# A pair's value product in three pieces among the scores, and fixed first-key tiles

## Chip, core and metric

The kernel runs on one core of a Trainium2 chip. The metric is device time in microseconds (us); lower is better. The engines of a core are TensorE (PE, matrix products; its weight loads are listed apart as PEld), VectorE (DVE), ScalarE (ACT), GpSimd (POOL) and SyncE (SP, which issues the DMAs here). Each engine works through its own list of instructions strictly in order and waits on semaphores for the others.

## What is computed

Three stages, all in float32; the attention stage is the one that the change touches.

```python
def _attn_ref(q, k, v, s):                 # q, k, v: (4, 8, 576, 64); s: (4, 8, 576)
    B, H, S, D = q.shape
    scores = q @ k.transpose(0, 1, 3, 2) / np.sqrt(D)
    causal = np.triu(np.ones((S, S), dtype=bool), k=1)
    cum = np.cumsum(np.maximum(s, 0.0), axis=-1)
    bias = -(cum[:, :, :, None] - cum[:, :, None, :])
    scores = np.where(causal, -1e9, scores + np.minimum(bias, 0.0))
    attn = softmax(scores)                 # max taken off, exp, divided by the row sum
    return attn @ v
# x = attn_out as (4, 576, 512)
# x = x + (u * (w_sg @ layernorm(v) + b_sg)) @ w_out, with (u, v) = gelu(x @ w_in)     (576, 1024)
# theta = x @ w_theta;  y = w_tok_r @ (x cos theta) + w_tok_i @ (x sin theta)
# out = (x + y) + relu((x + y) @ w_ch)
```

## The kernel before

**Stages.** The 32 heads (4 batches of 8) are worked through one after another by `attention`. After the eighth head of a batch, the first part of the feed-forward network of that batch (`ffn`) becomes the filler: `pace` emits pieces of it between the units of the next batch's heads, in proportion to their estimated cost in ns. So the first eight heads run without a filler (except loads of its weights), heads 8 to 31 with one. After head 31 come the rest of the network, the products with w_out, theta and the token mixing.

**One head.** A head has 576 queries in five tiles (0 to 4; tile 0 has 64 of its own) and the keys that each may see. `split_head` scales q and splits q and k into a rounded part and a remainder (tiles qA, kA, qB, kB; POOL, ACT and DVE share this work, and DMAs put the remainder and two rows of the running sum `cum` into qB and kB). `score_units` makes the scores of query tiles 0 to 3 in PSUM tiles of one bank (tag sc, four buffers) and those of tile 4 in a PSUM tile of two banks (sc2, one buffer, 288 columns used in each bank); then DVE takes the negated row maximum and ACT the exponential into E, with the row sums. `transpose_units` transposes E on PE (fifteen 128-column transposes in four PSUM tiles T, tag sc) and copies it out: the keys 0 to 63 to E0, the others to Ef. The product with the first key tile runs over 68 rows, of which rows 64 to 67 of E0 are zero; POOL sets them (L317) for every head, in a tile taken from a rotation of four.

**A pair.** Two heads share a tile of v. `pv_units` of an odd head makes the product of the pair: `R` and `R0` are the reciprocal row sums `Rb`, spread over the partitions by five transposes (ACT copies them to xT); `Y` (one bank) collects five key tiles for the queries 64 to 575, `Z` (64 columns) the one key tile of the first 64 queries. `pair` issues each product twice, once per head, the first head to the PSUM partitions 0 to 63 and the second to 64 to 127: the two are halves of the array that belong together. The five products of Y have 512, 512, 384, 128 and 256 columns. R0 and Z lie in spare columns of the last T. DVE multiplies Y and Z into xT (L376, L375), and `finish_pair` stores it and splits it for the network.

**What sets the order.** `ORDER` gives the units of one head in the order in which they are written: s a unit of scores of head g, t a unit of transposes of head g-1, p the split of head g+2 and the loads of head g+4; after them, in an even head, comes the whole `pv_units` of the pair before. When the kernel is built, a scheduler then puts each engine's instructions into a fixed order by their priority (the place in the program) and its own idea of when inputs and buffers are there. What runs is that order. The profile cuts buffer numbers and some endings from names: `sc` stands for sc and sc2, `E` for E and E0, `Q` and `K` for the loaded heads, and R0 and Z appear as T.

```python
    ORDER = "ssstsstspttt"
```

## Time and profile before

| | before |
|---|---|
| median of 3 runs | 723.15 us (719.99 to 725.91) |
| the profiled execution | 726.0 us |
| its span, first to last instruction | 723.9 us |
| PE, DVE, ACT, POOL busy in the span | 94%, 67%, 52%, 35% |
| mean granted TensorE clock | 0.983 of full speed |

The profile is of one execution, 0.4% above the median. A share of busy time is an average over stages: in the first 110 us there is no filler, from there to some 377 us attention and the network run together, then comes the change-over to the later stages.

### The profile page before, as it was taken

How to read it: one execution, taken by the hardware profiler on the slowest of the kernel's cores; microseconds unless marked ns; L12 is line 12 of the kernel's file. 1: busy time of each engine (PE TensorE's matmuls, PEld its weight loads, DVE VectorE, ACT ScalarE, POOL GpSimd, SP SyncE). 2: the span in 40 equal slices, each digit the busy share in tenths (PEclk: the TensorE clock that was granted, in tenths of full speed). 3: DMA queues.
4: the chain of work that ended last, by engine and by line, in shares of the span. 5: the costliest groups of instructions: out<-in, count | busy, mean ns of one | idle time of the engine just before them, and what ended most of it. 6: DMA issues, size and time to landing. Idle time of an engine off the chain costs nothing.

```text
span 723.9 us, 12514 instructions
## 1 busy us (share of the span) xinstructions
PE 678.8 (94%) x4496; PEld 593.8 (82%) x4496; DVE 486.4 (67%) x914; ACT 379.9 (52%) x888; POOL 254.0 (35%) x289
## 2 busy tenths in 40 slices
PE   6898978999999999999999687898999999999998
PEld 4676656888779878887788687887999989999997
DVE  5577979655659466675558899799876378457522
ACT  3567667764567734677436534566654056147100
POOL 6356544645326444454436654335000010010000
PEclk9999989999999999999999989999999999999999
DMA  5656763424332244321123578983100300300101
GB/s 143 192 158 186 202 174 91 114 73 141 108 99 78 77 122 144 110 69 42 42 93 119 176 240 260 326 290 124 66 1 1 132 1 1 126 6 1 66 1 65
DMA packets 50093, 80.76 MB, mean 112 GB/s; under 512 B 7248, under 2 KB 18768, under 8 KB 50032
## 3 DMA queue, kind: packets, MB, share of 16 engines
q1 hardware_dynamic: 50032, 79.97, 35.7%
q8 instruction: 35, 0.57, 0.3%
q14 instruction: 26, 0.21, 0.1%
HBM read 56.19 MB, written 19.02 MB: 104 GB/s over the span
## 4 chain that ended last, share of the span: by engine, by line
PE 60%; DVE 10%; DMA 4%; POOL 2%; issue 2%; ACT 2%; SPq 0%; DVEq 0%; POOLq 0%; ACTq 0%
PE yo L90 16%; PE fo L90 13%; PE co L90 7%; PE Y L90 6%; PE th L90 5%; PE sc L90 5%; PE T L329 4%; PE wo L90 2%; DVE wta L449 1%; DVE wta L451 1%; DMA x2d<-xr 1%; DMA x2T<-x2d 1%; DVE wta L448 1%; POOL vT L549 1%; DVE qA L245 1%
## 5 line engine op out<-in xcount | busy, mean ns | idle before, releaser
L282 ACT ACTIVATE E<-sc,negm 128x448 f32<-128x448 f32 (+4 forms) x160 | 84.2, 528 | 52.0 <-DVE negm L281 51.2
L281 DVE TENSOR_REDUCE negm<-sc 128x1 f32<-128x448 f32 (+4 forms) x160 | 74.2, 481 | 40.2 <-PE sc L90 39.0
L90 PE MATMUL yo<-wkh,zh 128*128 128x288 f32 x288 | 85.2, 296 | 0.1
L90 PE MATMUL yo<-wkl,zh 128*128 128x288 f32 x288 | 84.9, 296 | 0.0
L90 PE MATMUL yo<-wkh,zl 128*128 128x288 f32 x288 | 84.8, 296 | 0.0
L329 PE MATMUL T<-ident,E 128*128 128x128 f32 (+1 forms) x480 | 68.9, 277 | 3.3 <-ACT E L282 2.1
L90 PE MATMUL sc<-kA,qA 128*128 128x320 f32 (+3 forms) x192 | 63.0, 342 | 7.0 <-DVE Ef L335 3.2
L90 PE MATMUL sc<-kB,qB 68*128 68x320 f32 (+2 forms) x192 | 61.1, 328 | 6.6 <-DMA qB<-cd 3.1
L83 POOL TENSOR_SCALAR xt<-x2s 128x128 fp32r<-128x128 f32 x16 | 11.4, 725 | 136.7 <-PE tp L702 73.6
L90 PE MATMUL fo<-x,wih 128*128 128x288 f32 x256 | 58.4, 308 | 0.0
L329 PEld LDWEIGHTS T<-ident,E 128*128 128x128 f32 (+1 forms) x480 | 52.9, 133 | 6.4 <-ACT E L282 2.6
L245 DVE SCALAR_TENSOR_TENSOR qA<-Q,qA 64x576 fp32r<-64x576 f32 x32 | 48.5, 1516 | 10.5 <-POOL qA L243 9.8
L90 PEld LDWEIGHTS yo<-wkh,zh 128*128 128x128 f32 x288 | 54.1, 188 | 0.7 <-DVE x2T L775 0.4
L90 PEld LDWEIGHTS yo<-wkl,zh 128*128 128x128 f32 x288 | 53.9, 188 | 0.3
L90 PEld LDWEIGHTS yo<-wkh,zl 128*128 128x128 f32 x288 | 53.9, 188 | 0.1
L87 POOL TENSOR_TENSOR kB<-K,kA 64x576 fp32r<-64x576 f32 x32 | 49.9, 1559 | 8.9 <-ACT kA L79 7.2
L90 PE MATMUL co<-u,wch 128*128 128x288 f32 x256 | 52.9, 295 | 0.0
L90 PEld LDWEIGHTS sc<-kA,qA 128*128 128x128 f32 x192 | 37.1, 199 | 18.3 <-issue 5.6
L90 PE MATMUL wo<-gh,woh 128*128 128x288 f32 x128 | 39.8, 314 | 12.9 <-DVE xr L679 8.4
L90 PE MATMUL Y<-Ef,vr 128*64 128x128 f32 (+3 forms) x256 | 50.9, 439 | 0.0
L90 PEld LDWEIGHTS sc<-kB,qB 68*128 68x128 f32 x192 | 38.7, 202 | 9.2 <-issue 4.3
L317 POOL MEMSET E<- 4x576 f32 x32 | 17.4, 575 | 79.8 <-PE T L90 79.8
(172 smaller groups left out, 1938.4 us busy)
## 6 DMA issues: line engine op xcount, KB each, us to landing
Q<-in_q SPq DMA_DIRECT2D x64, 144.0 KB
K<-in_k SPq DMA_DIRECT2D x64, 144.0 KB
qB<-qA SPq DMA_DIRECT2D x32, 144.0 KB
xd<-xT SPq DMA_DIRECT2D x16, 288.0 KB
gd<-uT SPq DMA_DIRECT2D x16, 288.0 KB
gr<-gd SPq DMA_DIRECT2D x16, 288.0 KB
xr<-xd SPq DMA_DIRECT2D x16, 288.0 KB
x2d<-xr SPq DMA_DIRECT2D x16, 288.0 KB
```

What stands on the lines that cost most here:

```text
L83: nc.gpsimd.tensor_scalar(out, src, 1.0, 1.0, op0=ALU.mult, op1=ALU.mult)
L87: e.tensor_tensor(out, a, f32(hi), op=ALU.subtract)
L90: self.nc.tensor.matmul(out, lhsT, rhs, start=start, stop=stop)
L245: nc.vector.scalar_tensor_tensor(qA[64:128, :], Q2[64:128, :], 0.125, f32(qA[64:128, :]), op0=ALU.mult, op1=ALU.subtract)
L281: nc.vector.tensor_reduce(negm[0:rows, col:col + 1], o, axis=ax, op=ALU.max, negate=True)
L282: nc.scalar.activation(out, o, AF.Exp, bias=negm[0:rows, col:col + 1], accum_out=sm[0:rows, j, col:col + 1])
L317: nc.gpsimd.memset(E0[64:68], 0.0)
L329: nc.tensor.transpose(T[0:n, col:col + P], E[:, c:c + n], self.ident)
L448: nc.vector.tensor_scalar(ta.bitcast(U32), ta.bitcast(U32), 3, None, op0=ALU.logical_shift_left)
L449: nc.vector.scalar_tensor_tensor(ta.bitcast(U32), Hi, 0x80000000, ta.bitcast(U32), op0=ALU.bitwise_and, op1=ALU.bitwise_or)
L451: nc.vector.scalar_tensor_tensor(ta.bitcast(U32), L, 29, ta.bitcast(U32), op0=ALU.logical_shift_right, op1=ALU.bitwise_or)
L549: nc.gpsimd.tensor_scalar(vT[0:r, t], vT[0:r, t], rs[0:r, t:t + 1], nm[0:r, t:t + 1], op0=ALU.mult, op1=ALU.add)
```

## The change

The product of a pair moves from behind the even head that follows the pair to within the odd head after that, and is cut in three pieces, which `ORDER_V` places as v: R with its copy; the first two key tiles of Y; and R0, Z and the other three key tiles. The last pair of each batch stays where it was, in one go. R0 and Z now lie in spare columns (from 320) of the two banks of the head's own sc2 tile instead of in T. E0 is four fixed tiles; their rows 64 to 67 are set to zero once, by DVE, at the start, and the POOL instructions for it go.

```diff
+    ORDER_V = "sssvtsvstspvttt"
...
+        self.E0 = [self.a1.tile([P, S], F32, name=f"E0{i}") for i in range(4)]
...
+        for e in self.E0:
+            nc.vector.memset(e[64:68, :], 0.0)
...
-        o = self.psS.tile([P, 2, 512], F32, name="sc2", tag="sc2", bufs=1)
+        o = self.wide = self.psS.tile([P, 2, 512], F32, name="sc2", tag="sc2", bufs=1)
...
-        E0 = self.a2.tile([P, S], F32, name="E0", tag="E0", bufs=4)
+        E0 = self.E0[g % 4]
...
-        nc.gpsimd.memset(E0[64:68], 0.0)
...
     def pv_units(self, g):
...
-        R, R0 = self.psS.tile([P, 512], F32, name="R", tag="sc"), T[:, 384:512]
-        for t in range(5):
-            col = (t - 1) % 5
-            o = R0 if t == 0 else R[:, QS[t] - 64:QS[t] + 64]
-            nc.tensor.transpose(o, Rb[:, col].rearrange("p j d -> p (j d)"), self.ident)
-        nc.scalar.copy(xT[:, 512:576], R0[:, 0:64])
+        R = self.psS.tile([P, 512], F32, name="R", tag="sc")
+
+        def spread(o, t):
+            nc.tensor.transpose(o, Rb[:, (t - 1) % 5].rearrange("p j d -> p (j d)"), self.ident)
+
+        for t in range(1, 5):
+            spread(R[:, QS[t] - 64:QS[t] + 64], t)
         nc.scalar.copy(xT[:, 0:512], R)
-        yield 400.0
-
-        Y, Z = self.psS.tile([P, 512], F32, name="Y", tag="sc"), T[:, 320:384]
+        yield 300.0
+        Y = self.psS.tile([P, 512], F32, name="Y", tag="sc")
...
         pair(Y, 0, 68, 0, 0, 512, True, False)
+        pair(Y, 1, P, 0, 0, 512, False, False)
+        yield 1900.0
+
+        wide = self.wide
+        if wide is None:
+            wide = self.psS.tile([P, 2, 512], F32, name="sc2", tag="sc2", bufs=1)
+        Z, R0 = wide[:, 0, 320:384], wide[:, 1, 320:448]
+        spread(R0, 0)
+        nc.scalar.copy(xT[:, 512:576], R0[:, 0:64])
         pair(Z, 0, 68, 0, 512, 64, True, True)
-        yield 1100.0
-        for kt, a, c, n in ((1, 0, 0, 512), (2, 128, 512, 384), (4, 384, 896, 128), (3, 256, 1024, 256)):
+        for kt, a, c, n in ((2, 128, 512, 384), (4, 384, 896, 128), (3, 256, 1024, 256)):
             pair(Y, kt, P, a, c, n, False, kt == 3)
-            yield 1.8 * n
...
+            gp = g - 2 if (g - 2) % H != H - 1 else 0
+            pv = self.pv_units(gp) if gp > 0 and gp % 2 else iter(())
+            if g == n:
+                self.wide = None
+            for o in self.ORDER_V if gp > 0 and gp % 2 else self.ORDER:
...
+                c = next({"s": su, "t": tu, "v": pv}[o], None)
...
+            if g > 0 and g % H == 0:
                 self.run_units([self.pv_units(g - 1)])
```

What the scheduler makes of it is seen in the lists of instructions. First TensorE, at the second pair (heads 2 and 3). Before, its product stands in one go behind the transposes of head 3; `R` is R, `T<-ident,Rb` the transpose R0, and each `Y` row is one product or, with x2, one for each head:

```order
L356 MATMUL R<-ident,Rb 128x128 x4
L90 MATMUL Y<-E_487,vr 64x512
L90 MATMUL Y<-E_570,vr 64x512
L90 MATMUL Y<-Ef,vr 64x512 x2
L90 MATMUL Y<-Ef,vr 64x384
L356 MATMUL T<-ident,Rb 128x128
L90 MATMUL Y<-Ef,vr 64x384
L90 MATMUL Y<-Ef,vr 64x128 x2
L90 MATMUL Y<-Ef,vr 64x256 x2
```

After the change, in head 5; `sc_670` is that head's sc2 tile:

```order
L359 MATMUL R<-ident,Rb 128x128 x4
L359 MATMUL sc_670<-ident,Rb 128x128
L335 MATMUL T<-ident,E 64x128 x4
L93 MATMUL sc<-kA,qA 128x448
L93 MATMUL sc<-kB_73,qB_72 128x448
L93 MATMUL sc<-mask,identr 128x128
L93 MATMUL Y<-E_76,vr 64x512
L93 MATMUL Y<-E_77,vr 64x512
L93 MATMUL Y<-Ef,vr 64x512 x2
L93 MATMUL Y<-Ef,vr 64x384 x2
L93 MATMUL Y<-Ef,vr 64x128 x2
L93 MATMUL Y<-Ef,vr 64x256 x2
```

The transpose R0 has moved from between the two halves of the 384-column product to behind R, and the ten products of Y follow each other without anything between them.

Second, still TensorE, the rows that follow there; `sc_670<-E` are the two halves of Z, `T` the transposes of head 4, and `sc_769` is the sc2 tile of the next head:

```order
L93 MATMUL sc_670<-E_76,vr 64x64
L93 MATMUL sc_670<-E_77,vr 64x64
L335 MATMUL T<-ident,E 128x128 x10
L335 MATMUL T<-ident,E 64x128
L93 MATMUL sc<-kA,qA 128x64
L93 MATMUL sc<-kB_71,qB_70 128x64
L93 MATMUL sc<-mask,identr 128x64
L93 MATMUL sc_769<-kA,qA 128x288
```

Before, Z lay in T, and the sc2 tile of head 6 was filled among the score tiles of head 5, a head ahead; now its first product stands behind Z, which lies in the one buffer that both use.

Third, VectorE at the start of the program, where the running sum `cum` is made (sT, sh, sl, and on PE cumo; then cpos, two steps for each half of the columns) and the first two heads are split (qA). Before:

```order
L162 CAST tri<-trif 128x128
L123 CAST identr<-ident 128x128
L163 TENSOR_SCALAR sT<-sT 128x160
L164 CAST sh<-sT 128x160
L130 CAST mask<-maskf 128x128
L165 TENSOR_TENSOR sl<-sT,sh 128x160
L175 CAST cpos<-cumo 32x288
L176 TENSOR_TENSOR cpos<-cumo,cpos 32x288
L245 SCALAR_TENSOR_TENSOR qA<-Q_90,qA 64x576
L175 CAST cpos<-cumo 32x288
L176 TENSOR_TENSOR cpos<-cumo,cpos 32x288
L245 SCALAR_TENSOR_TENSOR qA<-Q_173,qA 64x576
```

After, from the last of the four new MEMSETs on, which stand ahead of the first CAST:

```order
L215 MEMSET E_77 4x576
L165 CAST tri<-trif 128x128
L126 CAST identr<-ident 128x128
L166 TENSOR_SCALAR sT<-sT 128x160
L133 CAST mask<-maskf 128x128
L167 CAST sh<-sT 128x160
L253 SCALAR_TENSOR_TENSOR qA<-Q_94,qA 64x576
L168 TENSOR_TENSOR sl<-sT,sh 128x160
L178 CAST cpos<-cumo 32x288
L179 TENSOR_TENSOR cpos<-cumo,cpos 32x288
L178 CAST cpos<-cumo 32x288
L253 SCALAR_TENSOR_TENSOR qA<-Q_181,qA 64x576
```

The four MEMSETs now stand ahead of sT, and each of the two qA operations has moved up by one place or more: the first ahead of sl, the second ahead of the last step of cpos, which follows the last row shown.

## Rows read from the trace of the kernel before

**Rows 1.** The page: the span, and PE's busy time, share and instructions.

```profile
span 723.9 us, 12514 instructions
...
PE 678.8 (94%) x4496; PEld 593.8 (82%) x4496; DVE 486.4 (67%) x914; ACT 379.9 (52%) x888; POOL 254.0 (35%) x289
```

**Rows 2.** Busy time per engine in two stretches; PEclk is the granted clock.

```profile
core 0: us, PE busy (x) PEld busy (x) DVE busy (x) ACT busy (x) POOL busy (x), PEclk, DMA share, GB/s
20.00:110.00 90.00, 77.85 (x469) 57.83 (x468) 66.97 (x121) 57.70 (x168) 47.69 (x47) 0.94 0.64 184
110.00:377.00 267.00, 260.92 (x1780) 217.10 (x1779) 168.09 (x300) 161.35 (x407) 124.87 (x140) 0.99 0.31 92
```

**Rows 3.** PE's timeline, one pair's product: start, length, instructions merged.

```profile
211.70 1.08 PE L90 MATMUL Y<-E,vr 68*64 68x512 f32 x4
212.60 1.67 PE L90 MATMUL Y<-Ef,vr 128*64 128x512 f32 x6
214.21 0.33 PE L356 MATMUL T<-ident,Rb 128*128 128x128 f32 x1
214.46 1.51 PE L90 MATMUL Y<-Ef,vr 128*64 128x384 f32 x10
215.90 0.30 PE L90 MATMUL sc<-kA,qA 128*128 128x64 f32 x1
```

**Rows 4.** The same view, another pair.

```profile
189.97 1.08 PE L90 MATMUL Y<-E,vr 68*64 68x512 f32 x4
...
193.13 0.30 PE L90 MATMUL sc<-kA,qA 128*128 128x64 f32 x1
...
193.74 0.65 PE L90 MATMUL Y<-Ef,vr 128*64 128x256 f32 x2
194.32 0.40 PE L90 MATMUL sc<-kA,qA 128*128 128x288 f32 x1
```

**Rows 5.** The same view, a third pair.

```profile
142.20 1.08 PE L90 MATMUL Y<-E,vr 68*64 68x512 f32 x4
...
144.07 0.33 PE L356 MATMUL T<-ident,Rb 128*128 128x128 f32 x1
144.32 2.37 PE L90 MATMUL Y<-Ef,vr 128*64 128x512 f32 x14
146.62 0.53 PE L90 MATMUL fo<-x,wih 128*128 128x288 f32 x2
```

**Rows 6.** DVE's timeline at the start of the program.

```profile
2.81 0.68 DVE L123 CAST identr<-ident 128x128 fp32r<-128x128 f32 x1 [0.31 <-POOL ident masks.py:199]
3.64 0.24 DVE L163 TENSOR_SCALAR sT<-sT 128x160 f32<-128x160 f32 x1 [0.15 <-DMA sT<-in_s]
...
7.97 0.75 DVE L245 SCALAR_TENSOR_TENSOR qA<-Q,qA 64x576 fp32r<-64x576 f32 x1 [0.42 <-POOL qA L243]
...
9.40 0.45 DVE L176 TENSOR_TENSOR cpos<-cumo,cpos 32x288 fp32r<-32x288 f32 x1
```

**Rows 7.** DVE's instruction groups before 30 us: busy, mean ns | idle before.

```profile
L465 DVE MEMSET wsrl<- 64x576 f32 x1 | 0.5, 538 | 0.2 <-issue 0.2
```

**Rows 8.** PE's timeline at the start.

```profile
12.47 0.39 PE L90 MATMUL sc<-kB,qB 68*128 68x64 f32 x1 [1.96 <-DMA qB<-cpos]
...
20.36 1.36 PE L329 MATMUL T<-ident,E 128*128 128x128 f32 x11
...
25.82 0.47 PE L90 MATMUL sc<-kA,qA 128*128 128x448 f32 x1 [1.69 <-DVE E L331]
```

**Rows 9.** POOL's waits: total us, times, longest.

```profile
POOL E L317 <- PE T L90: 79.8, 13, 9.7
```

**Rows 10.** PE's waits, three of them.

```profile
PE T L90 <- ACT xT L357: 1.0, 1, 1.0
...
PE sc L90 <- POOL kB L87: 0.7, 1, 0.7
...
PE sc L90 <- DVE qA L245: 0.6, 1, 0.6
```

**Rows 11.** DVE's timeline behind one pair's product.

```profile
50.72 0.69 DVE L376 TENSOR_TENSOR xT<-Y,xT 128x512 f32<-128x512 f32 x1 [2.77 <-PE Y L90]
...
51.96 0.23 DVE L375 TENSOR_TENSOR xT<-T,xT 128x64 f32<-128x64 f32 x1
```

More of the change, by code (lines that the diff above doesn't have):

```diff
@@ L339, in transpose_units @@
             yield 440.0 if i < 3 else 330.0
-        self.ET[g] = (E0, Ef, T)
+        self.ET[g] = (E0, Ef)
     def pv_units(self, g):
-        if g % 2 == 0:
-            return
         nc = self.nc
-        (A0, Af, _), (B0, Bf, T) = self.ET.pop(g - 1), self.ET.pop(g)
+        (A0, Af), (B0, Bf) = self.ET.pop(g - 1), self.ET.pop(g)
         vr = self.vop[g // 2]
-        xT = self.xT = self.f2.tile([P, S], F32, name="xT", tag="xT")
+        xT = self.f2.tile([P, S], F32, name="xT", tag="xT")
         Rb = self.Rb.pop(g // 2)
-        R, R0 = self.psS.tile([P, 512], F32, name="R", tag="sc"), T[:, 384:512]
-        for t in range(5):
-            col = (t - 1) % 5
-            o = R0 if t == 0 else R[:, QS[t] - 64:QS[t] + 64]
-            nc.tensor.transpose(o, Rb[:, col].rearrange("p j d -> p (j d)"), self.ident)
-        nc.scalar.copy(xT[:, 512:576], R0[:, 0:64])
+        R = self.psS.tile([P, 512], F32, name="R", tag="sc")
[3 more added lines that the diff above has]
+            spread(R[:, QS[t] - 64:QS[t] + 64], t)
         nc.scalar.copy(xT[:, 0:512], R)
-        yield 400.0
-        Y, Z = self.psS.tile([P, 512], F32, name="Y", tag="sc"), T[:, 320:384]
+        yield 300.0
+        Y = self.psS.tile([P, 512], F32, name="Y", tag="sc")
         def pair(o, kt, rows, a, c, n, start, stop):
@@ L368, in pv_units @@
         pair(Y, 0, 68, 0, 0, 512, True, False)
+        pair(Y, 1, P, 0, 0, 512, False, False)
[6 more added lines that the diff above has]
+        nc.scalar.copy(xT[:, 512:576], R0[:, 0:64])
         pair(Z, 0, 68, 0, 512, 64, True, True)
-        yield 1100.0
-        for kt, a, c, n in ((1, 0, 0, 512), (2, 128, 512, 384), (4, 384, 896, 128), (3, 256, 1024, 256)):
+        for kt, a, c, n in ((2, 128, 512, 384), (4, 384, 896, 128), (3, 256, 1024, 256)):
             pair(Y, kt, P, a, c, n, False, kt == 3)
-            yield 1.8 * n
         nc.vector.tensor_tensor(xT[:, 512:576], Z, xT[:, 512:576], op=ALU.mult)
         nc.vector.tensor_tensor(xT[:, 0:512], Y, xT[:, 0:512], op=ALU.mult)
+        self.xT = xT
         self.finish_pair(g)
-        yield 0.0
+        yield 1700.0
     def finish_pair(self, g):
@@ L409, in attention @@
         for g in range(n + 1):
-            if g < n:
-                su = self.score_units(g)
-                tu = self.transpose_units(g - 1) if g > 0 else iter(())
-                order = self.ORDER
-                for o in order:
-                    if o == "p":
-                        if g + 2 < n:
-                            self.split_head(g + 2)
-                        if g + 4 < n:
-                            self.load_head(g + 4)
-                        if g % 2 and g + 3 < n:
-                            self.load_v(g + 3)
-                        continue
-                    c = next(su if o == "s" else tu, None)
-                    if c is not None:
-                        self.pace(c)
-            else:
-                self.run_units([self.transpose_units(g - 1)])
-            if g > 0:
-                self.run_units([self.pv_units(g - 1)])
-                if g % H == 0:
-                    b = g // H - 1
-                    if b < B - 1:
-                        self.drain()
-                        self.fill = self.ffn(b)
+            su = self.score_units(g) if g < n else iter(())
+            tu = self.transpose_units(g - 1) if g > 0 else iter(())
+            gp = g - 2 if (g - 2) % H != H - 1 else 0
[3 more added lines that the diff above has]
+            for o in self.ORDER_V if gp > 0 and gp % 2 else self.ORDER:
+                if o == "p":
+                    if g + 2 < n:
+                        self.split_head(g + 2)
+                    if g + 4 < n:
+                        self.load_head(g + 4)
+                    if g % 2 and g + 3 < n:
+                        self.load_v(g + 3)
+                    continue
+                c = next({"s": su, "t": tu, "v": pv}[o], None)
+                if c is not None:
+                    self.pace(c)
+            if g > 0 and g % H == 0:
+                self.run_units([self.pv_units(g - 1)])
+                b = g // H - 1
+                if b < B - 1:
+                    self.drain()
+                    self.fill = self.ffn(b)
     def split64(self, src, rows, raw, ta, his, lo, sub):
```

## The prediction

> **What bounds the kernel now.** The page comes first: PE is busy 678.8 of 723.9 us, far more than any other engine [rows 1]. A share over the whole span says little, so I next read the busy time by stretch [rows 2]. From 110 to 377 us, where attention and the filler run together, PE is busy 260.92 of 267 us: 6.1 us idle, 2.3%. There PE is the bound, and a microsecond taken from its work comes off the end. From 20 to 110 us, the first heads without a filler, it is busy 77.85 of 90 us: 12.15 us idle, 13.5%, at a granted clock of 0.94. Here the waits have a share. So I ask two things of the change: does it take work from PE, and what does it do to the waits.
>
> PE's timeline answers the first. In [rows 3] the first two products of 512 columns, one per head, take 0.90 us from their start to that of the next (211.70 to 212.60). The reader should see what stands in the middle of Y: at 214.21 the transpose R0, with 384-column products on both sides. By the order it parts the two halves of the 384-column pair. Two halves that stand next to each other run at the same time, two that are parted run one after the other, and the rows give the price. Without what lies between, Y takes 2.51 + 1.44 = 3.95 us here; 3.16 + 0.58 = 3.74 us where the 256-column pair is parted [rows 4]; and 1.87 + 2.30 = 4.17 us where a 512-column pair is [rows 5]. The work is the same, only the parted pair differs: 0.43 us for 256 columns more, 1.68 ns a column. A parted pair thus costs 0.86 us at 512 columns, 0.645 at 384 and 0.43 at 256, and an unparted Y would take 3.31 us in all three places.
>
> **The change part by part.** *The pieces.* In the order before, each of the 16 products of Y is parted once: ten at 384 columns, four at 256, two at 512. That is 6.45 + 1.72 + 1.72 = 9.9 us of PE time. In the order after the change, five are: three at 384, one at 256, one at 512, or 1.93 + 0.43 + 0.86 = 3.2 us; and three times the two 64-column halves of Z are parted, 0.11 us each by the same rate, 0.3 us. **PE does 9.9 - 3.5 = 6.3 us less work** (unrounded). Of that, 1.8 us lie in the first four pairs, where a wait could take their place; the other 4.5 us lie in the stretch that PE bounds. The transposes and products are otherwise the same in number and size. Six products of Y are now cut between two pairs, which parts nothing, and R0 mostly stands beside R; I take no gain or loss from that, with 1 us either way.
>
> *The zero rows at the start.* POOL loses 32 MEMSETs, DVE gains four. None of DVE's four is in the trace; the nearest row is the MEMSET of the same 576 columns, 0.538 us [rows 7], so 2.15 us. They stand ahead of sT, which heads the chain to the first complete scores: sT, sh, sl, the cumo products on PE, cpos, and its DMA, for which PE waits until 12.47 us [rows 8]. DVE has little slack there, 0.31 us before identr and 0.15 us before sT [rows 6]: the chain starts 1.7 us later. The new order also puts the first qA operation (0.75 us, [rows 6]) ahead of sl, and the second ahead of the last step of cpos, which ended at 9.85 us before: up to 1.5 us more. So the first complete scores come 1.7 to 3.2 us later. Not all of it need arrive: before 25.82 us PE waits 1.69 us for DVE's copy of E [rows 8], and what DVE does ahead of that copy hangs on the loads of a later head, which SP issues nearly as early as before. I take **2.0 us lost**, between 0.5 and 3.2.
>
> The Trainium skill, VectorE: DVE Perf Modes, section on zero memsets, says that a memset takes a cycle per element; by its 0.96 GHz that is an estimate of 0.60 us for 576 columns, 2.4 us for four, and a loss of 2.2 us instead of 2.0 us. The trace's row is a little shorter, and it is used.
>
> *The zero rows later.* The MEMSET made POOL wait 79.8 us for PE, up to 9.7 us at a time [rows 9]; behind it in POOL's queue stood the qA and kB splits for the head after next, and behind these the DMAs of qB and kB. It sounds like much, but POOL is off the path: of PE's waits those that lead to the splits are 0.7 us on kB and 0.6 us on qA, and 1.0 us more was Z waiting for ACT's copy of R0 out of the same T [rows 10], which now lie in different banks. Of these 2.3 us I take **1.0 us gained**; bounds 0 and 2.3.
>
> *The filler.* The first product of the network stands behind 269 rows of PE's list instead of 230, about one head later, some 10 us (an estimate: nine heads in the 90 us of the first stretch). One head more at 13.5% idle instead of 2.3% is 1.1 us; I take **0.5 us lost**, between 0 and 1.1. The network's work itself is neither more nor less; some 25 of its products stand behind the last pair that stood ahead of it before.
>
> *Waits that are added.* Each odd head's sc2 tile is held until DVE has multiplied Z, and the next head's sc2 products stand behind that on PE, with everything after them. DVE's two products took 0.69 and 0.23 us [rows 11]; between Z and the next sc2 tile PE has eleven transposes, 1.36 us [rows 8], and one small score tile. So the wait is covered if DVE comes to these products on time. Nothing else is counted for it; if that cover is gone it is the third rival. R, and the new Rb that has to wait for R0, sit a head away from their use.
>
> Sum against the profiled execution: 726.0 - 6.3 + 2.0 - 1.0 + 0.5 = 721.2 us. The median of the runs is 723.15, a factor 0.9961 of it, so the forecast for a median is **718.4 us**, 0.7% less.
>
> **The rivals.** *First: the waits go too.* While PE made the product of a pair, DVE stood idle 2.77 us before it could multiply [rows 11], and then had the reductions, copies and splits of the next head all at once. If the product within a head gives them a cover, most of the 12.15 us idle from 20 to 110 us [rows 2] may go; two thirds, less the 1 us already counted, is 7 us: 711 us. For it speaks that the last T transposes are now preceded by 3.3 us of PE work; against it, that some of that idle time belongs to loads of weights and DMAs, which the change leaves where they are.
>
> *Second: the start eats it.* If the start's 3.2 us arrive in full, the first pairs' 1.8 us vanish in waits, and the 1.0 us does not come, 726.0 - 4.5 + 3.2 + 0.5 = 725.2 profiled, 722.4 us as a median: no change. For it: the stretch before 110 us is the one where PE waits. Against it: the idle time before 25.82 us.
>
> *Third, the slower end: the sc2 buffer becomes the wait.* Before, a head's sc2 tile was filled a head ahead; now fifteen times it waits for DVE's product of Z. If DVE comes to it 1 us later than the cover lasts (the qA split of the head after next, 0.75 us in [rows 6], and the row sums for Rb, which need the head's last exponential, stand ahead of it in its queue), 15 us come on top: 733 us. It decides from 0.32 us a pair, where it has eaten the forecast's 4.8 us. For it: one buffer, and an in-order PE. Against it: DVE is busy only 63% between 110 and 377 us [rows 2].
>
> The Trainium skill, PSUM — Partial Sum Buffer, section on bank collisions, has the rule that access is to be guarded by bank and quadrant, not by address: Z in columns that the scores don't use frees nothing, which is this rival. No row of before shows the sc2 buffer shared in this way.
>
> **How the numbers follow.** Forecast (718.4, give or take 3): 0.50. First rival (711): 0.20. Second (722.4): 0.20. Third (733): 0.08; something else, 0.02. The likeliest gives the time, 718.4. One percent, about what a measurement of this kernel tells from no change, is 715.9 to 730.4. Faster than that: nine tenths of the first rival and a third of the forecast, 0.35. Slower: most of the third, 0.05. The rest, 0.60, is within. The range leaves out the far half of the first rival and the third: 710.5 to 725.5.
>
> **What the profile will show.** Right: PE's Y products take 3.3 us a pair where unparted; PE's busy time is some 6 us less; the first scores with kB start at 14 to 16 us; POOL has no MEMSET for E. Wrong, if PE's wait before the sc2 products on DVE's xT sums to over 4 us, if parted and unparted pairs take the same, or if the stretch from 377 to 520 us, which is not bounded by PE alone and whose DVE order is shuffled, moves by more than 3 us.

## The result, and the profile after

The changed kernel takes 712.2 us (median; 711.9 to 713.0) where the kernel before, in the same comparison, takes 723.6 us: ratio 0.983, 95% interval 0.981 to 0.986, or 11.4 us less. The forecast was 718.4 us, 0.7% less. The profiled execution after is one of 712.5 us.

The page after:

```profile
span 710.7 us, 12461 instructions
...
PE 666.2 (94%) x4496; PEld 586.9 (83%) x4496; DVE 479.1 (67%) x918; ACT 378.5 (53%) x888; POOL 234.1 (33%) x257
```

PE's busy time is 12.6 us less than in [rows 1], twice what was forecast. Its idle time is the same: 44.5 us of 710.7, against 45.1. So what was gained is work of PE, and the extra gain is work too. Of the 12.6 us, 10.5 lie ahead of the last 262 products of the network (341.8 us against 352.4, at a mean granted clock of 0.98 in both). The other 2.1 us lie behind, where the change takes out no work; in the change-over there the clock was 0.98 against 0.96.

The busy time by stretch, as in [rows 2] (cut at 364.20 us, where as much of the network is left as at 377.1 us before):

```profile
20.00:110.00 90.00, 81.71 (x530) 61.94 (x530) 73.21 (x136) 61.20 (x192) 45.22 (x41) 0.94 0.66 189
110.00:364.20 254.20, 249.88 (x1733) 210.30 (x1731) 156.96 (x294) 159.43 (x396) 110.94 (x118) 0.99 0.33 98
```

From 110 us on PE is idle 4.3 us, before it was 6.1. From 20 to 110 us it is idle 8.3 us; before it was 12.2, but 8.6 in a second profile of the same kernel (before_again, below).

PE's timeline, one pair's product, to be set beside [rows 3 to 5]:

```profile
48.25 1.08 PE L93 MATMUL Y<-E,vr 68*64 68x512 f32 x4
49.16 2.32 PE L93 MATMUL Y<-Ef,vr 128*64 128x512 f32 x16
51.32 0.28 PE L93 MATMUL sc<-E,vr 68*64 68x64 f32 x4
51.53 1.42 PE L335 MATMUL T<-ident,E 128*128 128x128 f32 x11
```

From 48.25 to 51.32 us all ten products of Y follow each other: 3.07 us. The two halves of Z (`sc<-E,vr`) are behind them, then come the transposes. Another pair, one of the five whose halves are parted:

```profile
208.32 1.08 PE L93 MATMUL Y<-E,vr 68*64 68x512 f32 x4
209.23 1.67 PE L93 MATMUL Y<-Ef,vr 128*64 128x512 f32 x6
210.83 0.66 PE L335 MATMUL T<-ident,E 128*128 128x128 f32 x4
211.42 1.51 PE L93 MATMUL Y<-Ef,vr 128*64 128x384 f32 x10
212.86 0.33 PE L335 MATMUL T<-ident,E 128*128 128x128 f32 x1
```

Four transposes lie between the two halves of 384 columns. Without them Y takes 2.51 + 1.44 = 3.95 us, just what it took in [rows 3]. A parted pair of 384 columns thus costs 3.95 - 3.07 = 0.88 us, not the 0.645 us of the prediction.

A cut between two products, which parts no halves, costs something as well. The Y that starts at 229.91 us is cut so twice, by R0 at 231.78 us and by four transposes at 232.83 us; without these it takes 1.87 + 0.79 + 0.80 = 3.46 us, some 0.2 us more for each cut.

PE's timeline at the start, answering to [rows 8]:

```profile
15.75 0.40 PE L93 MATMUL sc<-kB,qB 68*128 68x64 f32 x1 [3.17 <-DMA qB<-cpos]
...
27.77 0.27 PE L93 MATMUL sc<-kB,qB 68*128 68x64 f32 x1 [0.61 <-DMA qB<-cd]
```

and DVE's, answering to [rows 6]:

```profile
2.15 2.36 DVE L215 MEMSET E<- 4x576 f32 x4 [0.16 <-issue]
...
6.11 0.76 DVE L253 SCALAR_TENSOR_TENSOR qA<-Q,qA 64x576 fp32r<-64x576 f32 x1 [0.61 <-POOL qA L251]
...
12.66 0.45 DVE L179 TENSOR_TENSOR cpos<-cumo,cpos 32x288 fp32r<-32x288 f32 x1
```

The four MEMSETs take 2.36 us, 0.59 each, against the 0.538 of [rows 7]. The first scores with kB start at 15.75 us instead of 12.47, 3.3 us later. The estimate of 0.60 us that the prediction made from the Trainium skill, VectorE: DVE Perf Modes, section on zero memsets, was nearer than the row.

POOL's waits, answering to [rows 9]:

```profile
POOL qA L251 <- PE sc L93: 54.6, 21, 8.6
```

The 79.8 us for E are gone, but POOL now waits 54.6 us before qA, for PE's scores of the head that still reads the tile (28.0 us before the change). The wait has moved one instruction on. Of PE's waits in [rows 10] those for kB and qA are gone, and that for ACT's copy to xT now stands ahead of Y:

```profile
PE Y L93 <- ACT xT L363: 1.7, 1, 1.7
```

### The profile page after: what moved, and what is told of

It is laid out like the page before. It is cut to its first block, busy times and chain, and to the rows that moved or that the text cites. A ratio compares the mean times of both kernels' runs of the same rounds, so it can differ in the third digit from the quotient of the medians.

```text
span 710.7 us, 12461 instructions
## 1 busy us (share of the span) xinstructions
PE 666.2 (94%) x4496; PEld 586.9 (83%) x4496; DVE 479.1 (67%) x918; ACT 378.5 (53%) x888; POOL 234.1 (33%) x257
## 4 chain that ended last, share of the span: by engine, by line
PE 69%; DVE 9%; DMA 8%; ACT 5%; issue 3%; SPq 3%; POOL 2%; ACTq 0%; DVEq 0%; POOLq 0%
PE yo L93 16%; PE fo L93 14%; PE sc L93 8%; PE Y L93 7%; PE co L93 7%; PE th L93 6%; PE T L335 6%; PE wo L93 3%; DMA wraw<-in_moe_w_in 2%; DVE wta L461 1%; DMA gt<-in_moe_w_sg 1%; DMA x2T<-x2d 1%; ACT E L290 1%; PE tp L714 1%; DVE wta L463 1%
## 5 line engine op out<-in xcount | busy, mean ns | idle before, releaser
L290 ACT ACTIVATE E<-sc,negm 128x64 f32<-128x64 f32 (+4 forms) x160 | 84.1, 529 | 43.3 <-DVE negm L289 42.4
L289 DVE TENSOR_REDUCE negm<-sc 128x1 f32<-128x64 f32 (+4 forms) x160 | 73.8, 482 | 37.9 <-PE sc L93 36.7
L335 PE MATMUL T<-ident,E 128*128 128x128 f32 (+1 forms) x480 | 70.7, 278 | 1.9 <-ACT E L290 1.7
L93 PE MATMUL sc<-kA,qA 128*128 128x64 f32 (+3 forms) x192 | 64.0, 343 | 5.8 <-ACT E L290 2.5
L93 PE MATMUL sc<-kB,qB 68*128 68x64 f32 (+3 forms) x192 | 60.6, 322 | 3.8 <-DMA qB<-cpos 3.2
L86 POOL TENSOR_SCALAR xt<-x2s 128x128 fp32r<-128x128 f32 x16 | 10.9, 696 | 144.7 <-DVE x2s L90 144.7
L93 PE MATMUL fo<-wih,x 128*128 128x512 f32 x128 | 44.3, 406 | 2.1 <-ACT wih L82 1.4
L93 PE MATMUL Y<-Ef,vr 128*64 128x128 f32 (+3 forms) x256 | 46.0, 467 | 0.0
L251 POOL TENSOR_SCALAR qA<-Q 128x576 fp32r<-128x576 f32 x32 | 22.4, 699 | 69.1 <-PE sc L93 54.6
L93 PEld LDWEIGHTS fo<-x,wih 128*128 128x128 f32 x256 | 42.4, 188 | 1.8 <-issue 1.2
```

Source lines behind the costliest of these rows:

```text
L86: nc.gpsimd.tensor_scalar(out, src, 1.0, 1.0, op0=ALU.mult, op1=ALU.mult)
L93: self.nc.tensor.matmul(out, lhsT, rhs, start=start, stop=stop)
L251: nc.gpsimd.tensor_scalar(qA, Q2, 0.125, 1.0, op0=ALU.mult, op1=ALU.mult)
L289: nc.vector.tensor_reduce(negm[0:rows, col:col + 1], o, axis=ax, op=ALU.max, negate=True)
L290: nc.scalar.activation(out, o, AF.Exp, bias=negm[0:rows, col:col + 1], accum_out=sm[0:rows, j, col:col + 1])
L335: nc.tensor.transpose(T[0:n, col:col + P], E[:, c:c + n], self.ident)
```

## The experiments

Theory A: the gain is PE's work on the product of a pair, because halves stand together and R0 is outside. The rivals are:

- B: POOL no longer waits behind its MEMSET.
- C: the product among the scores covers waits.
- D: the scheduler's order has shifted elsewhere by chance.
- E, added later: the place of the fixed tiles moves the order behind the last head.

All times are medians, all ratios to the kernel before on the same chip.

| run | median, us | ratio | 95% interval |
|---|---|---|---|
| zero_only | 714.7 | 0.988 | 0.985 to 0.991 |
| pieces_only | 709.5 | 0.981 | 0.978 to 0.985 |
| zero_pool | 712.8 | 0.985 | 0.982 to 0.988 |
| behind | 714.4 | 0.988 | 0.985 to 0.991 |
| start_only | 721.1 | 0.996 | 0.994 to 0.998 |
| zero_late | 715.9 | 0.989 | 0.985 to 0.993 |
| wide_only | 707.9 | 0.977 | 0.974 to 0.981 |
| before_again | 722.9 | 1.001 | 0.998 to 1.003 |
| headwise | 746.2 | 1.032 | 1.028 to 1.035 |
| zero_each | 718.5 | 0.992 | 0.990 to 0.994 |
| r0_only | 697.1 | 0.963 | 0.961 to 0.965 |
| wide_zero | 705.4 | 0.974 | 0.972 to 0.977 |
| r0_zero | 697.8 | 0.964 | 0.961 to 0.967 |
| zero_each2 | 717.5 | 0.992 | 0.989 to 0.995 |

### The two parts of the change, each alone

*zero_only*: before, with the zero rows as in the change.

```diff
+        self.E0 = [self.a1.tile([P, S], F32, name=f"E0{i}") for i in range(4)]
...
+        for e in self.E0:
+            nc.vector.memset(e[64:68, :], 0.0)
...
-        E0 = self.a2.tile([P, S], F32, name="E0", tag="E0", bufs=4)
+        E0 = self.E0[g % 4]
...
-        nc.gpsimd.memset(E0[64:68], 0.0)
```

> Before, with only the zero rows changed: four fixed E0 tiles, zeroed once by DVE at the start, no MEMSET on POOL; the product of a pair stays where it was, in one go, with R0 and Z in T. Theory A (the gain is PE work of the pair: halves no longer parted, R0 no longer between products): all sixteen Y are still parted by the order (five at 256 columns, nine at 384, one at 512, one at 128... at most 1 us less than before), so PE's busy time stays within 2 us of 678.8 and the later first scores cost 1 to 3 us: 723 to 726 us, ratio 0.999 to 1.004. Theory B (a good part of the gain is POOL's splits and their DMAs coming earlier, since nothing waits behind a MEMSET any more): the idle time of PE from 20 to 110 us falls by some 4 us from 12.2, and the time comes to 719 to 721 us, ratio 0.994 to 0.997.

Measured 714.7 us, faster than either theory had it: 8.3 us for a part that the prediction had put at a loss of 1 us.

*pieces_only*: after, with the same lines taken the other way.

> After, with the zero rows as before: E0 in a rotation of four, MEMSET on POOL in every head, none on DVE at the start; the product in three pieces, R0 and Z in the sc2 tile. Theory A: PE's busy time stays at about 666 us, the first scores with kB come at 12.5 us again, and the time is that of after less 1 to 3 us: 709 to 711.5 us, ratio 0.980 to 0.983. Theory B: the waits of PE before 110 us are back, 4 us more idle than after there, and the start's 3 us are saved: 712 to 715 us, ratio 0.984 to 0.988.

Measured 709.5 us: theory A, which had counted the later start's 1 to 3 us as saved here. The pieces alone bring 13.5 us, more than the whole change. So the parts do not add (8.3 + 13.5 against 11.4), and the gain of the zero rows is not there when the pieces are.

### The start, and the place of the pieces

*zero_pool*: after, with POOL zeroing each fixed tile once.

```diff
-        for e in self.E0:
-            nc.vector.memset(e[64:68, :], 0.0)
...
         E0 = self.E0[g % 4]
+        if g < 4:
+            nc.gpsimd.memset(E0[64:68], 0.0)
```

> After, but the four fixed E0 tiles are zeroed by POOL, each when its first head's transposes are written, instead of by DVE at the start. Where the later start arrives in full (3.3 us at the first scores with kB): 709 to 710 us, ratio 0.979 to 0.981. Where it is eaten by the next waits (for E, for loads): 711.5 to 712.5 us, ratio 0.983 to 0.985, with as much more idle time of PE between 20 and 30 us as is saved ahead of it.

Measured 712.8 us: nothing is gained by the earlier start. PE's timeline of this run shows what became of it up to the first Y (the last row):

```profile
12.49 0.39 PE L93 MATMUL sc<-kB,qB 68*128 68x64 f32 x1 [1.95 <-DMA qB<-cpos]
...
25.68 0.47 PE L93 MATMUL sc<-kA,qA 128*128 128x448 f32 x1 [1.40 <-DVE E L337]
27.06 0.27 PE L93 MATMUL sc<-kB,qB 68*128 68x64 f32 x1 [0.91 <-DMA qB<-cd]
...
35.32 1.08 PE L93 MATMUL Y<-E,vr 68*64 68x512 f32 x4
```

The scores start 3.3 us earlier than after the change; then PE waits 1.40 us for DVE's copy of E and 0.91 for qB, where after the change it waits 0.61 us in all, and its first Y starts at 35.32 us against 35.48. Of 3.3 us 0.2 are left. But the waits took only part of it. From the first scores with kB to the first Y, in this run and after the change (columns as in [rows 2]):

```profile
12.49:35.32 22.83, 19.85 (x102) 17.60 (x103) 16.13 (x31) 15.24 (x48) 8.98 (x10) 0.93 0.67 186
```

```profile
15.75:35.48 19.73, 18.03 (x102) 15.67 (x102) 14.88 (x30) 14.30 (x47) 7.49 (x9) 1.00 0.66 184
```

For the same 102 instructions PE is idle 2.98 us against 1.70, and busy 19.85 us against 18.03: it was at 1.2 GHz from 27.6 to 31.1 us, where after the change the clock was full. So of the 3.1 us 1.3 are waits and 1.8 the clock. Nor does the run change the start alone: TensorE's order in the attention differs from that of the change (8 blocks instead of 11 in the count below). It does not show that a later start costs nothing, and pieces_only, which starts as early, is 2.7 us under the change (the intervals overlap).

*behind*: after, with the pieces behind the last transposes of the head.

```diff
-    ORDER_V = "sssvtsvstspvttt"
+    ORDER_V = "ssstsstsptttvvv"
```

> After, with the three pieces behind the last transposes of the odd head instead of among its scores; only the order of writing differs. By its order thirteen Y are unparted, R0 stands beside R. Theory A (what counts is that the halves stand together and R0 outside, not where the product stands): Y 3.1 to 3.3 us where unparted, PE busy within 2 us of 666, time 711 to 714 us, ratio 0.983 to 0.987. Theory C (what counts is that PE has 3 us of other work within the head while E is copied out and the row maxima are made): PE's idle time before the end of attention is 5 us or more above after's, time 716 to 720 us, ratio 0.990 to 0.995.

Measured 714.4 us, between the two ranges. The interval overlaps that of the change: the place among the scores is worth some 2 us, not told from nothing, and theory C does not carry the gain. But it has a part. PE's idle time up to the last 262 products of the network is 28.8 us against 22.4, more than the 5 us that C asked for, and at the same time its work is less (one batch, below, has 88.5 us of it against 91.2). Standing among the scores saves waits, and costs about as much in work.

### What the zero rows gained alone

*start_only*: before, with four MEMSETs more on DVE at the start.

```diff
+        self.pad = self.a1.tile([P, S], F32, name="pad")
...
+        for e in range(4):
+            nc.vector.memset(self.pad[64:68, :], 0.0)
```

> Before, with four MEMSETs of DVE more at the start (576 columns, into a tile that nothing reads), and nothing else: POOL's MEMSETs stay in every head. It takes apart what the zero rows alone did, 0.988. Theory B (POOL's splits and their DMAs come earlier, since nothing waits behind a MEMSET): the gain does not come here, 723 to 726 us, ratio 1.000 to 1.004. Theory D (the later start moves the scheduler's order in the heads 10 to 14 and in the change-over behind the last head, and that order is the better one; POOL has no part in it): the gain comes here as well, 713 to 717 us, ratio 0.986 to 0.992.

*zero_late*: before, with the fixed tiles, zeroed by POOL for the first four heads (the lines of zero_pool).

> Before, with four fixed E0 tiles that POOL zeroes for the first four heads, each where the MEMSET stood; from head 4 on no MEMSET. TensorE's order differs from that of before in two dozen small places only, and the start is that of before. Theory B (POOL): the gain of the zero rows comes here, 713 to 717 us, ratio 0.986 to 0.992. Theory D (the scheduler's order): it does not, 721 to 724 us, ratio 0.997 to 1.001.

*before_again* (no edit):

> The kernel before, once more, for a second profile. If the stretches of the granted clock at 1.2 GHz belong to the kernel's order, they stand again at 27, 99, 126, 406, 416 and 433 us, and the profiled time is some 726 us. If they differ from execution to execution, they stand elsewhere, and the profiled time lies between 720 and 727 us with the number of them: about 1.6 us for each 3.4 us at that clock.

start_only gave 721.1 us, 0.4% less, between the two ranges: not all of it is POOL's, and not all of it order. TensorE's order differs from that of before in the attention, and is the same behind it; that the order brings the 0.4% is not shown. zero_late gave 715.9 us, which spoke for B. In before_again the granted clock was at 1.2 GHz near 27, 98, 125, 405 and 435 us, as in the first profile of before, but at 74 us and from 12 to 23 us too, and not at 416 us (the first profile has no record of the clock ahead of 20 us); the execution took 722.5 us against 726.0. The first profile, against which the prediction's sum was made, was a long one, by idle time: 45.1 us against 40.2.

*zero_each*: before, with the fixed tiles, and POOL's MEMSET kept in every head.

```diff
-        E0 = self.a2.tile([P, S], F32, name="E0", tag="E0", bufs=4)
+        E0 = self.E0[g % 4]
...
         nc.gpsimd.memset(E0[64:68], 0.0)
```

> Before, with four fixed E0 tiles in place of the rotation of four, and the MEMSET on POOL kept in every head: the work is that of before, only where the tiles lie differs, and with it, behind the last head, TensorE's order in the products with w_out and the transposes tp in two dozen places, as with the zero rows alone. Theory B (POOL's MEMSET with its wait is what the zero rows save): the gain of 0.988 does not come, 721 to 724 us, ratio 0.997 to 1.001. Theory E (the place of the tiles and the order behind the last head that goes with it): the gain comes, 714 to 717 us, ratio 0.987 to 0.992.

*zero_each2* (the same):

> Fixed E0 tiles in before with POOL's MEMSET in every head, once more. Theory E: 716 to 719 us again, ratio 0.990 to 0.994; in the second profile the stretch from the first to the last third of the change-over (first product with w_out to first product of the token mixing) takes 99 to 102 us again, and the batches ahead of it 94.5 us from pair 8 to pair 12, as before. If the first result was chance: 721 to 724 us.

718.5 (between the two ranges) and 717.5 us: 0.992 twice, though POOL waits 74.5 us for E, much as before (79.8 us). The work is that of before; the tiles lie elsewhere, and TensorE's order differs behind the last head alone. With start_only's 0.996 the product is 0.988, zero_only's ratio; no run has the two of them without the rest. The stretch from the last 262 products of the network to the first product of the token mixing, before:

```profile
377.10:519.30 142.20, 125.39 (x776) 113.79 (x774) 124.25 (x257) 78.34 (x165) 64.63 (x70) 0.96 0.64 207
```

and in zero_each:

```profile
374.90:509.70 134.80, 122.77 (x776) 112.73 (x775) 120.32 (x257) 78.44 (x165) 64.64 (x70) 0.97 0.65 217
```

142.2 against 134.8 us; PE's busy time differs by 2.6 and its idle time by 4.8 us. (In the second profiles of the two it is 139.9 and 136.5 us.)

### Where R0 and Z lie

*wide_only*: before, with R0 and Z in the sc2 tile, the product in one go where it was.

```diff
+        o = self.wide = self.psS.tile([P, 2, 512], F32, name="sc2", tag="sc2", bufs=1)
...
-        R, R0 = self.psS.tile([P, 512], F32, name="R", tag="sc"), T[:, 384:512]
+        wide = self.wide if g + 1 < B * H else self.psS.tile([P, 2, 512], F32, name="sc2", tag="sc2", bufs=1)
+        R, R0 = self.psS.tile([P, 512], F32, name="R", tag="sc"), wide[:, 1, 320:448]
...
-        Y, Z = self.psS.tile([P, 512], F32, name="Y", tag="sc"), T[:, 320:384]
+        Y, Z = self.psS.tile([P, 512], F32, name="Y", tag="sc"), wide[:, 0, 320:384]
```

> Before, with R0 and Z in spare columns of the sc2 tile of the even head after the pair; the product in one go where it was, E0 and its MEMSETs as before. By the order R0 stands outside Y, five Y have no parted pair, the others are parted at 256 columns (six), 384 (three) or 512 (one, which is parted at 128 too), and Z is parted eleven times. Theory A (PE work of the pair): by 2.0 ns a column, as after the change, Y takes 57 to 58 us instead of 62.8 and R 2 us less: PE busy some 6 to 7 us under 678.8, time 715 to 718 us, ratio 0.989 to 0.994. Theory C (what counts is where the product stands among the scores): 721 to 725 us, ratio 0.997 to 1.002, the work of PE saved coming back as waits.

Measured 707.9 us, better than the whole change, and more than A gave it.

*r0_only*: the same for R0 alone (`wide` as there); Z stays in T.

```diff
-        R, R0 = self.psS.tile([P, 512], F32, name="R", tag="sc"), T[:, 384:512]
+        R, R0 = self.psS.tile([P, 512], F32, name="R", tag="sc"), wide[:, 1, 320:448]
```

> Before, with R0 alone in spare columns of the sc2 tile; Z stays in T, E0 and its MEMSETs as before. By the order R0 stands outside Y, three Y have no parted pair, four are parted by scores and Z at 256 columns or by nothing, nine by the two halves of Z. If only a full-width operation in between parts a pair (theory A as it now reads: a half runs beside whatever the other half of the array does), Y takes 52 to 54 us in all, as in the run with both moved, and the time is 707 to 711 us, ratio 0.977 to 0.983. If two halves of Z in between part it as well (the first of them has to wait for the half of Y ahead of it, and the other half of Y behind that), Y takes 58 to 60 us, R 2 us less, and the time is 715 to 719 us, ratio 0.989 to 0.994.

Measured 697.1 us: 26 us less than before, twice the gain of the change, and below what either reading gave. PE's timeline of one pair shows the reading that holds:

```profile
223.44 0.60 PE L357 MATMUL R<-ident,Rb 128*128 128x128 f32 x4
223.97 1.08 PE L90 MATMUL Y<-E,vr 68*64 68x512 f32 x4
224.88 1.34 PE L90 MATMUL Y<-Ef,vr 128*64 128x512 f32 x5
225.75 0.33 PE L90 MATMUL T<-E,vr 68*64 68x64 f32 x2
225.92 0.81 PE L90 MATMUL Y<-Ef,vr 128*64 128x384 f32 x3
226.39 0.28 PE L90 MATMUL T<-E,vr 68*64 68x64 f32 x2
226.50 0.87 PE L90 MATMUL Y<-Ef,vr 128*64 128x128 f32 x8
227.31 0.40 PE L90 MATMUL fo<-x,wih 128*128 128x288 f32 x1
```

Both halves of Z (`T<-E,vr`) lie between the two halves of the 384-column product, and Y and Z together take 3.34 us, as they do where nothing parts Y after the change (48.25 to 51.53, 3.28 us). An operation of half the array's width in between parts nothing. In its profile PE is busy 660.2 us and idle 34.8, where before it was 678.8 and 45.1 (680.2 and 40.2 in the second profile): most of the gain is work, the rest waits. Moving R0 has changed the scheduler's order too, and Z now stands within Y.

*wide_zero* and *r0_zero*: wide_only and r0_only with the lines of zero_late added.

> Before, with R0 and Z in the sc2 tile and, besides, four fixed E0 tiles that POOL zeroes for the first four heads; the product in one go where it was. It is meant as the better version. If the two gains (0.977 and 0.989) add up: 700 to 703 us, ratio 0.966 to 0.972. If the zero rows save nothing where the product's place has already shortened POOL's wait for E (27 us in place of 80 with R0 and Z moved): 706 to 709 us, ratio 0.976 to 0.980.

> Before, with R0 alone in the sc2 tile (0.963) and, besides, four fixed E0 tiles that POOL zeroes for the first four heads, none after that. TensorE's order behind the last head is that of the run with R0 alone, and it differs from it in three places of one product each. Theory E (what the zero rows saved was the order behind the last head, which R0 alone has brought as well): no gain on top, 695 to 699 us, ratio 0.961 to 0.966. Theory B (POOL's waits for E cost time in every batch): 688 to 692 us, ratio 0.952 to 0.957.

705.4 and 697.8 us. The first is 2.5 us under wide_only (the intervals overlap), and it has the order behind the last head that zero_each has. The second tells B and E apart: r0_zero has the fixed tiles, keeps r0_only's order there, takes only POOL's MEMSETs away, and gains nothing. So neither the MEMSETs nor the place of the tiles by itself brings the gain; that leaves the order. POOL's wait, again, has only moved:

```profile
POOL qA L245 <- PE sc L90: 43.8, 12, 12.0
```

(25.7 us before qA and 41.1 us before E in r0_only.)

### Double the suspected cost

*headwise*: after, with the five products of one head in the second piece and those of the other in the third (`head(i)` makes the five of one head).

```diff
...
-        pair(Y, 0, 68, 0, 0, 512, True, False)
-        pair(Y, 1, P, 0, 0, 512, False, False)
+        head(0)
         yield 1900.0
...
-        for kt, a, c, n in ((2, 128, 512, 384), (4, 384, 896, 128), (3, 256, 1024, 256)):
-            pair(Y, kt, P, a, c, n, False, kt == 3)
+        head(1)
```

> After, with the ten products of Y in another order: the second piece makes the five of the first head, the third R0, Z and the five of the second head. The same products, only the halves that stood together stand apart in all sixteen pairs (the last of the first head and the first of the second run at the same time where nothing is between them). Theory A (a half costs its columns at 1.7 ns where the other half of the array has nothing to do at the time): Y takes 5.5 to 6.0 us a pair instead of 3.1, PE is busy 38 to 46 us more, and the time is 748 to 758 us, ratio 1.035 to 1.048. Rival (what cost time in the middle of Y was the change to the transpose and back, not that the halves stood apart): Y stays at 3.1 to 3.4 us and the time within 4 us of 712, ratio 0.982 to 0.990.

Measured 746.2 us, 34 us over the change, 2 us under A's range, far from the rival's. PE's timeline of one pair:

```profile
348.81 1.07 PE L93 MATMUL Y<-E,vr 68*64 68x512 f32 x2
349.72 2.32 PE L93 MATMUL Y<-Ef,vr 128*64 128x512 f32 x8
351.97 0.66 PE L335 MATMUL T<-ident,E 128*128 128x128 f32 x4
352.56 0.34 PE L93 MATMUL sc<-E,vr 68*64 68x64 f32 x4
352.73 1.02 PE L93 MATMUL Y<-E,vr 68*64 68x512 f32 x2
353.59 2.32 PE L93 MATMUL Y<-Ef,vr 128*64 128x512 f32 x8
355.84 0.40 PE L93 MATMUL fo<-x,wih 128*128 128x288 f32 x1
```

The five products of one head take 3.16 us (348.81 to 351.97), those of the other 3.11 us (352.73 to 355.84): each as long as all ten together in the change.

### One batch of each kernel

From the Y of pair 8 to that of pair 12 lies the same work in every kernel, at the full clock, and where a kernel's profile was taken twice the stretch came out within 0.05 us. The rows of before, after and r0_only:

```profile
211.70:306.18 94.48, 93.41 (x639) 77.87 (x638) 60.76 (x106) 57.24 (x149) 45.01 (x51) 1.00 0.35 103
```

```profile
208.32:300.36 92.04, 92.01 (x643) 77.95 (x642) 57.74 (x106) 58.11 (x147) 39.30 (x43) 1.00 0.36 106
```

```profile
201.21:288.74 87.53, 87.53 (x637) 76.46 (x636) 57.63 (x107) 58.32 (x149) 44.41 (x51) 1.00 0.38 111
```

Set beside it is a count: how often in this stretch PE goes over from full-width operations to the half-width products of Y and Z (a block is a run of them with nothing else between). A Y is parted where full-width work stands between the two halves of one of its products. Busy times are put on 264 products of the network, at 0.17 us each, where a kernel has some more in the stretch (after 5, pieces_only 7, zero_pool 9, headwise 5).

| | blocks | parted Y, of four | PE busy, us | idle, us |
|---|---|---|---|---|
| before | 13 | 4 | 93.4 | 1.1 |
| after | 11 | 2 | 91.2 | 0.0 |
| wide_only | 9 | 1 | 90.5 | 1.2 |
| pieces_only | 8 | 1 | 89.4 | 0.0 |
| zero_pool | 8 | 1 | 89.4 | 0.0 |
| behind | 7 | 0 | 88.5 | 1.2 |
| r0_only | 4 | 0 | 87.5 | 0.0 |
| headwise | 9 | all halves apart | 100.9 | 0.1 |

Headwise apart, PE's work falls with the number of blocks, from 93.4 us at 13 to 87.5 at 4, one to a pair. By the differences from r0_only a block more goes with 0.3 to 0.65 us, parted halves included. The row of behind tells the two apart:

```profile
217.53:307.23 89.70, 88.46 (x637) 76.44 (x637) 58.75 (x108) 56.96 (x150) 39.59 (x43) 1.00 0.37 109
```

In this stretch of behind, as in that of r0_only, no half of Y or Z is parted from its other half by full-width work. So the 0.9 us between them are the price of going over three times more, 0.3 us a block. By this estimate the nine blocks more of before are 2.8 us of its 5.9 us over r0_only, and its four parted Y the other 3.1, or 0.77 us each. The same two prices give 91.2 us for after and 89.5 for pieces_only and zero_pool, close to what was measured; wide_only, where some halves of Z stand alone, is 0.7 us above them. The Trainium skill, TensorEngine Tiling (Array Packing), section Key Properties, says that a change of tiling mode drains TensorE; it has no price. The 0.3 us a block agree with it; that they are a drain no row shows.

## Why the prediction fell short

**The bound and the mechanism held.** PE is the bound; taking work from its product of a pair shortens the kernel; parted halves run one after the other (headwise). Up to the last 262 products of the network PE's busy time is 341.8 us, against 352.4 and 354.4 in the two profiles of before (the second with a mean granted clock of 0.96 there, the others 0.98), and its idle time 22.4 us against 24.7 and 21.5. That stretch is 12.9 and 11.7 us shorter; what follows it takes 346.5 us against 346.8 and 344.5. The gain is all in the attention, and all or nearly all of it is work.

**The step that failed is the first term, "PE does 6.3 us less work": it was mis-sized, and measured 10.5 to 12.6 us (10.5 at equal clocks).** Two assumptions of it were wrong.
- The price of a parted pair was taken from three parted pairs alone, as a line through zero, 1.68 ns a column, which made an unparted Y 3.31 us. It takes 3.07 us in the row shown. The slope was right: headwise parts all 1792 columns of Y, 3.01 us by the slope, and its Y takes 3.16 + 3.11 - 3.07 = 3.20 us more. But each parting also costs some 0.24 us that does not go with the columns, about what a cut between two whole products costs. It was in all three rows alike, so their differences could not show it. Over the eleven Y that are no longer parted this is 2.6 us.
- "R0 mostly stands beside R; I take no gain or loss from that" and "cut between two pairs, which parts nothing": both touch what I did not price, PE's going over between full-width and half-width work. R0 stood in the middle of 15 of the 16 Y, and stands there in three after the change (at 155.00, 171.32 and 231.78 us). In the middle it took 0.25 us ([rows 3], 214.21 to 214.46), as one of four beside each other 0.13 (r0_only, 223.44 to 223.97): for twelve of them some 1.4 us by this estimate. Against it stand the new cuts, some 0.2 us each. On balance 13 blocks of the batch above became 11, and r0_only, with 4, shows what was left lying.

**The start, 2.0 us lost: not settled.** The chain came 3.3 us later, at the upper end (3.2), as the new order of DVE gave it. Whether that reaches the end no run shows by itself. Without the four MEMSETs at the start the time is 0.6 us longer (zero_pool) or 2.7 us shorter (pieces_only); with them alone in before it is 1.9 us shorter (start_only); and TensorE's order in the attention differs in each. The argument that the next waits take up part of it held: up to the first Y they took 1.3 us in zero_pool, one of them that of [rows 8].

**POOL's zero rows, 1.0 us gained: nothing in r0_zero.** The wait moved from the MEMSET to the next instruction that needs the same head finished. That POOL is off the path was right. (zero_late is 1.6 and 2.6 us under the two runs of the tiles alone, and their intervals overlap: that much at most.) That the zero rows alone gain 8 us had another cause, which the prediction did not have: with fixed tiles the scheduler's order behind the last head is another (zero_each, 5 and 6 us), and the four MEMSETs at the start bring 2 us (start_only), for which the order that they move in the attention is the likely cause, but not shown. The change has an order of its own there, the same with and without the fixed tiles (pieces_only), and so nothing of this gain.

**The filler, 0.5 us lost**, cannot be told apart in any run.

**The rivals.** *The waits go too* came out near the time (711) with the wrong mechanism: PE's idle time of 44.5 us stands against 45.1 and 40.2 before, and from 20 to 110 us, where the rival looked, it is 8.3 us against 12.2 and 8.6. *The start eats it*: the gain of work was not eaten; the most that any run puts on the start is 2.7 us (pieces_only). *The sc2 buffer becomes the wait*: no wait of PE for DVE's product stands ahead of sc2. DVE comes at once, answering to [rows 11]:

```profile
51.53 0.69 DVE L387 TENSOR_TENSOR xT<-Y,xT 128x512 f32<-128x512 f32 x1
52.14 0.21 DVE L386 TENSOR_TENSOR xT<-sc,xT 128x64 f32<-128x64 f32 x1
```

**What the profile was to show.** Y at 3.3 us where unparted: 3.07. PE some 6 us less busy: 12.6, 10.5 of it in the attention. First scores with kB at 14 to 16 us: 15.75. No MEMSET of E on POOL: right. The stretch behind the attention was to move by under 3 us: it is 144.7 us against 142.2 and 139.9, 2.5 to 4.8 us longer, and the stage behind it 2.8 us shorter (201.8 against 204.6); work went over from one to the other.

**What stays open.** Why the order behind the last head that the fixed tiles bring is the better one, and whether the change would gain from it, was not tried. What the later start costs was not isolated from the order that moves with it, and the change was not tried with Z back in T.

## What to carry to other kernels

A price worked out from the differences of like cases lacks whatever they all share; look for one row of the other case (here a single product whose halves stand together) before multiplying it by sixteen. Where products use half of the array, keep all of them in one block: no full-width operation, and not even a small transpose, should stand in it; here moving that one transpose (R0), with the order that the scheduler then made, gave 26 us, more than twice the whole change. When a wait goes from an engine off the path, ask what its next instruction waits for; and when only buffers move, compare the scheduled order of the stages that seem to have nothing to do with it.

## What the runs showed of the hardware

Two half-width products in the two halves of the array overlap even if they are not of the same size or tensor: a half of Z runs beside a half of Y (r0_only, where Y and Z together take 3.34 us, against 3.28 where Z follows Y). Parted by full-width work, the halves run one after the other: the five products of one half alone take as long as all ten together (headwise, 3.16 and 3.11 us against 3.07). And going over to half-width work and back costs TensorE some 0.3 us even where nothing is parted (behind against r0_only).

The granted clock took a share that these edits did not aim at. After the change it was at 1.2 GHz here, behind stretches in which PE was partly idle (columns as in [rows 2]):

```profile
78.00:84.00 6.00, 3.17 (x23) 2.62 (x23) 5.88 (x8) 5.47 (x17) 4.14 (x4) 1.00 0.46 140
84.00:91.00 7.00, 6.55 (x37) 5.83 (x36) 7.00 (x14) 4.97 (x14) 4.22 (x4) 0.76 0.75 221
91.00:98.00 7.00, 4.45 (x30) 3.58 (x32) 6.35 (x14) 5.00 (x18) 1.75 (x3) 0.99 0.78 201
98.00:104.70 6.70, 6.70 (x24) 2.65 (x24) 6.02 (x8) 3.18 (x9) 4.42 (x4) 0.50 0.30 80
```

and one whole product of a pair fell into it:

```profile
97.94 1.97 PE L93 MATMUL Y<-E,vr 68*64 68x512 f32 x4
99.70 4.48 PE L93 MATMUL Y<-Ef,vr 128*64 128x512 f32 x16
104.11 1.24 PE L335 MATMUL T<-ident,E 128*128 128x128 f32 x7
```

6.17 us instead of 3.07. Such stretches come in every profile, only partly in the same places, and executions of one kernel differ by some 1% (719.7 to 728.0 us for before). How much of that is the clock is not shown: of the two profiles of before, the one at the lower mean clock (0.973 against 0.983) was the shorter.
